# Four more filler products in batch 1's first unit, and the last softmax sums moved behind two more filler products and copied out by ScalarE

## The chip, the cores and the metric

The kernel runs on one core of one Trainium2 chip. The metric is the device time of one execution in microseconds, and less is better. Before the change it takes 974.06 us (median of 3 runs, 973.99 to 974.19). One execution was also recorded by the hardware profiler: its span is 971.3 us, and all times below that are given as a place ("at 526 us") count from the start of that span.

## The reference

Two blocks are computed one after the other, in float32. First comes attention over 4 batches, 8 heads, 768 positions and head size 64, in which a query sees only the keys that were assigned to the same one of 16 centroids:

```python
q_assign = argmax(einsum('bhsd,hcd->bhsc', q_n, c_n)); k_assign = argmax(...)   # normalized q, k, centroids
mask   = q_assign[:, :, :, None] == k_assign[:, :, None, :]
scores = where(mask, q @ k^T / sqrt(D), -1e9)
attn   = exp(scores - max) / (sum + 1e-9);  out = attn @ v
```

Its output, as 3072 tokens of width 512 (heads side by side), goes through a feed-forward block:

```python
h = x @ w_in            # 512 -> 2048
g = maximum(h, 0) ** 2
y = g @ w_out           # 2048 -> 512
```

## The kernel before, in words

**Two stages.** The first stage (up to 531 us) does all of the attention, and, mixed into it, the feed-forward block of batch 0. The second stage (531 us to the end) does the feed-forward block of batches 1 to 3 with seven products in place of eight (`ffn_pair`, a scheme of sums and differences of quarter matrices).

**Attention.** Heads go in pairs: `pair` counts 16 of them, four to a batch (`HP = 4`), and `h` is the half of the queries (384 columns). A unit is (pair, h, c), where c is 0, 2 or 4 and stands for two chunks of 128 keys. There are 96 units, run in the loop over `u`: the first 24 belong to batch 0, and so unit 24 is batch 1's first. A unit makes scores on TensorE (`scores`, tiles `sc`, lines 91 and 94) and the exponential on ScalarE (line 479). In batch 0 the mask is a second product on TensorE. From batch 1 on, VectorE multiplies by the mask (line 483): it compares `qid`, the cluster numbers of the queries, spread over all partitions, with `ids`, those of the keys, and writes `ex`. The tiles `sc` have two buffers of two banks each, and each unit uses both, so that the scores of one unit wait until the masks of the unit before have read the bank. GpSimd adds the `ex` tiles into `acc` (lines 493 and 495), and TensorE multiplies them with v (`times_v`, tiles `av`).

**Sums and division.** When a half is complete, `add_up` lets TensorE sum `acc` over partitions (`sm`), takes the reciprocal on VectorE into `r` (line 554), writes it to DRAM (`far_r`, line 557), reads it back to all partitions (`rb`, line 560), and also stores it in `seen`, from which `check_sums` learns at the end of attention whether all sums were in range. Then `finish` multiplies `av` by `rb` into `xT` (line 573), the input of the feed-forward block. In batch 0's second halves ScalarE copies the sums from their bank into `r` before the reciprocal (line 552); everywhere else the reciprocal reads the bank.

**Filler.** The feed-forward block of batch 0 is computed with plain products (`ffn`, a generator): 64 products of 384 columns per half for the first matrix (`ph`, line 587; ScalarE's relu and square to `gT` follow) and 48 of 512 columns for the second (`po`, line 600, then an output copy `osb` by ScalarE and a DMA). `fill_steps` takes them from the generators while TensorE would otherwise wait. How many a unit gets follows from `left`, the columns still to do, and `density(u)`, the weight of a unit: the share of a step is the columns left, less `RESERVE = 3 * DM`, times the weights of the step, over the weights of all units to come. Seven plain `po` products are left when the last unit's `av` products are done.

**Order.** Each engine runs its own list in order. The lists are made by a scheduler from the order of the program, from priorities (`tc.high_priority`) and from `tc.issue_after`. A change in the counts of filler products can therefore also move instructions of other engines past each other, such as the DMAs on SyncE's queue. On that queue stand, for each pair, the write of the transposed cluster numbers (`far<-row`, line 415), their spread to all partitions (`qid<-far`, line 416), and the DMA that transposes the next pair's q and k (`qkT<-words`, line 293).

**Other work beside it.** Up to about 160 us the feed-forward weights are loaded and rounded (`round_weights`, lines 150 to 167) by ScalarE, VectorE and GpSimd. The second stage begins with sums of inputs (`x_t`) and of `w_out` (`w_t1` to `w_t4`, 2048 columns each) on VectorE, and of `w_in` (`w_s`, 256 columns each) on GpSimd. Its products go to eight banks in turn; VectorE's additions into `g` (line 649) empty them. The eight banks take over those of the first stage, the one of the last `sm` among them.

Of the kernel before, what the change touches and what calls it, by code (L numbers as in the profile page):

```python
# [25 lines left out]
def kernel(  # L26
# [14 lines left out]
    NCH = S // P  # L41
    DM = H * D
# [3 lines left out]
    HP = H // 2  # L46
    NB = NCH // 2
    TB = NB * P
    NG = B * HP
# [31 lines left out]
    def bank(name, shape):  # L81
        return ps_f.tile(shape, F32, name=name, tag="f")
# [5 lines left out]
    def together(products, offset=2000):  # L88

        products = iter(products)  # L90
        last = nc.tensor.matmul(**next(products))  # L91
        with tc.high_priority(offset=offset):
            for product in products:
                last = nc.tensor.matmul(**product)  # L94
        return last.ins
# [178 lines left out]
    def split_words(pair, which):  # L274
        if which == 0:
            words[pair] = dram.tile([2 * NCH, P, 2, 2 * D], U16, name="words")
        flat = loads.tile([P, NCH, 2, 2 * D], U16, name="flat", tag="qk")
        src = raw[pair][which].bitcast(U16).rearrange("p c (d two) -> p c two d", two=2)
        half = NCH // 2
        with tc.issue_after(last_exp[0]):  # L280
            for cols in (slice(0, half), slice(half, NCH)):
                nc.scalar.copy(out=flat[:, cols], in_=src[:, cols])
        nc.sync.dma_start(
            words[pair][NCH * which : NCH * (which + 1)].rearrange("c p two d -> p c two d"),
            flat,
        )
        if which == 1:
            raw.pop(pair)
            load_qk(pair + 1)
# [131 lines left out]
    def prep(pair):  # L421
        if pair < HP:
            return [
                lambda: turn(pair, 0), lambda: turn(pair, 1), lambda: turn(pair, 2),
                lambda: logits(pair), lambda: route(pair),
                lambda: turn_onehot(pair, 0), lambda: turn_onehot(pair, 1),
            ]

        split = [lambda i=i: split_words(pair + 1, i) for i in range(2 if pair + 1 < NG else 0)]
        first, second = split or (None, None)  # L430
        return [
            lambda: turn_words(pair), None, None, first, None, None,
            lambda: logits(pair), None, lambda: route(pair), second, None, None,
            None, None, lambda: spread(pair),
        ]
# [10 lines left out]
    def first_half(pair, h):  # L446
        return pair < HP and h == 0
# [51 lines left out]
    def ones_products(sm, e, rhs, first, last):  # L499

        n, rows = TB // 2, P // 4
        return [
            dict(
                out=sm[rows * (2 * e + g) : rows * (2 * e + g + 1)], lhsT=ups[:, 0:rows],
                rhs=rhs[:, n * g : n * (g + 1)], start=first, stop=last,
            )
            for g in range(2)
        ]
# [27 lines left out]
    def add_up(pair, h):  # L536


        b, hp = divmod(pair, HP)
        if first_half(pair, h):  # L540
            sm = sums.pop((pair, h))
            nc.scalar.copy(out=xT_of(b, h)[:, hp], in_=av.pop((pair, h)))
        else:
            total = acc.pop((pair, h))
            sm = bank("sm", [P, TB // 2])
            one = [ones_products(sm, e, total[:, e], True, True) for e in range(2)]
            together([p for both in zip(*one) for p in both])
        row = 4 * (2 * pair + h)
        r = once.tile([P, TB // 2], F32, name="r")
        if pair < HP and h:  # L550

            nc.scalar.copy(out=r, in_=sm)
            sm = r
        nc.vector.reciprocal(out=r, in_=sm)
        r = r.rearrange("(r p) n -> r p n", r=4)[:, 0]
        far = dram.tile([2, TB], F32, name="far_r")
        nc.sync.dma_start(far.rearrange("e (g n) -> (e g) n", g=2), r)
        rb = rbp.tile([P, TB], F32, name="rb", tag="rb")
        for e in range(2):
            nc.sync.dma_start(rb[D * e : D * (e + 1)], far[e].partition_broadcast(D))  # L560
        nc.sync.dma_start(seen[row : row + 4], r)
        spread_out[pair, h] = rb

    def xT_of(b, h):
        if (b, h) not in xT:
            pool = {0: xtp, 1: xt_first, 2 * B - 1: xtp}.get(2 * b + h) or later["xT"]
            xT[b, h] = pool.tile([P, KT, TB], F32, name="xT")
        return xT[b, h]
# [44 lines left out]
    def ffn_pair(pools, b):  # L613
# [114 lines left out]
    units = [  # L728
        (pair, h, c)
        for pairs, halves in [(range(HP), [0]), (range(HP), [1])]  # L730
        + [([pair], [0, 1]) for pair in range(HP, NG)]
        for pair in pairs for h in halves for c in range(0, NCH, 2)
    ]
# [10 lines left out]
    def density(u):  # L744


        return 4 if u < HP * NCH else 2 if u < len(units) - NCH else 3

    def fill_steps(columns):

        while fill and columns > 0:
            if (passed := next(fill[0], None)) is None:
                fill.pop(0)
            else:
                columns -= passed
                left[0] -= passed

    def behind_first(u, what=last_logits):
        return tc.issue_after(what[0]) if u == 0 else ExitStack()

    def next_pair(u):

        pair, h, c = units[u]
        if c == 0 and pair + 1 < NG and h == 0 and (pair + 1) not in qkT:
            if pair + 1 < HP or pair >= HP:
                return pair + 1
        if u == TWOS + 4:
            return HP
        return None
# [26 lines left out]
    for u in range(len(units) + 3):  # L796
        if u < len(units):
            pair, h, c = units[u]
            if (p := next_pair(u)) is not None:
                ahead.extend(prep(p))  # L800
            if u in (TWOS, TWOS + 2):

                split_words(HP, int(u > TWOS))
            if c == 0 and u + 3 < len(units) and units[u + 3][0] not in raw_v:
                load_v(units[u + 3][0])

            with behind_first(u):
                scores(pair, h, c)

        ends(added)  # L810
        added.clear()
        if u < TWOS:
            ready = u - 1
        elif u == TWOS or u % 2 or u >= len(units):
            ready = u

        complete, late = late, []
        while v_next < min(ready, len(units)):
            pair, h, c = units[v_next]
            times_v(pair, h, c)  # L820
            v_next += 1
            if c == NCH - 2:
                (late if h and not HP * NCH <= u < len(units) else complete).append((pair, h))
        for pair, h in complete:
            with tc.high_priority(offset=1000) if first_half(pair, h) else ExitStack():
                add_up(pair, h)
            if h == 1:
                for d in (qkT, ids, qid):
                    d.pop(pair)
            if h == 1 or pair < HP:  # L830
                raw_v.pop(pair)
            added.append((pair, h))

        rounding += 4
        while rounding >= 3:
            rounding -= 3
            i = next(to_round, None)
            if i is not None:
                with tc.issue_after(last_exp[0]):
                    round_weights(i)  # L840
                if (i := next(loaded, None)) is not None:
                    load_weights(i)
            elif not later:
                early.close()
                for name, bufs in (("xT", 5), ("out", 2)):
                    later[name] = keep.enter_context(
                        tc.tile_pool(name=name + "_late", bufs=bufs, side="right",
                                     reuse_waits="tile")
                    )
        share = 0  # L850
        if u % 2 == 0 or not TWOS < u < len(units):
            n = 2 if TWOS < u < len(units) else 1
            share = max(0, left[0] - RESERVE) * sum(map(density, range(u, u + n)))
            share //= max(1, sum(map(density, range(u, ENDS))))
        goal = left[0] - share

        for i in range(3):
            if i == 2:
                fill_steps(share * 2 // 3)
            if ahead:  # L860
                with behind_first(u, masked if i else last_logits):
                    (ahead.pop(0) or int)()
        fill_steps(left[0] - goal)
# [235 lines left out]
```

The softmax here doesn't subtract the row's maximum and nothing guards it: scores larger than these inputs give would overflow.

## Time and profile before

The time is 974.06 us and the span in the profile 971.3 us, at a granted TensorE clock of 1.00 throughout. The table shows how long TensorE was busy in stretches of the span. What is missing to the length of the stretch is idle time.

| Stretch, us | Length | TensorE busy | What runs there |
|---|---|---|---|
| 0 to 20 | 20.0 | 15.69 | loads, centroids, first routing |
| 20 to 60 | 40.0 | 39.05 | first halves of batch 0 |
| 140 to 160 | 20.0 | 18.40 | last unit of batch 0, first units of batch 1 |
| 200 to 240 | 40.0 | 39.24 | batch 1, with filler |
| 400 to 440 | 40.0 | 39.34 | batch 3, with filler |
| 440 to 480 | 40.0 | 39.58 | batch 3, with filler |
| 510 to 531 | 21.0 | 19.41 | last unit, last sums, last filler |
| 531 to 603 | 72.0 | 72.00 | second stage, batch 1, first matrix |
| 893 to 971.3 | 78.3 | 72.67 | second stage, batch 3, second matrix, and output |

The stretches between, which are not shown, have 0.3 us of idle time in all. In a row of the timeline the columns are the start, the duration, the engine, the line, the operation, what is written from what is read, its shape and its count, and in brackets how long the engine had been idle before it and what ended that. A row of the waits names who waited for whom, the total in microseconds, how many times, and the longest. SPq rows are DMAs as SyncE's queue issues them. TensorE shows each float32 product as two records, so "x4" of line 600 is two products.

### The profile page before, as it was taken

What the parts mean: (1) busy time and instruction counts of PE and PEld (TensorE: products, weight loads), DVE (VectorE), ACT (ScalarE), POOL (GpSimd) and SP (SyncE); (2) the same over time, 40 slices, a digit from 0 to 9 for tenths busy, and PEclk for the clock granted to TensorE, in tenths of its full rate; (3) what the DMA queues carried; (4) which work ended last, traced back from release to release, by engine and by line L of the source; (5) the groups of instructions that cost most, each with busy time, mean ns of one, the idle gap of its engine ahead of it and who ended that gap; (6) DMA issues with size and microseconds to landing.
All of it is one profiled execution on the core that took longest, in us unless ns stands there. A gap on an engine that the chain in (4) does not pass through costs nothing.

```text
span 971.3 us, 12075 instructions
## 1 busy us (share of the span) xinstructions
PE 955.1 (98%) x4479; PEld 550.6 (57%) x4479; DVE 569.1 (59%) x913; ACT 316.8 (33%) x516; POOL 381.8 (39%) x277
## 2 busy tenths in 40 slices
PE   7999999999999999999999999999999999999997
PEld 4544454443444444443444556888556888556886
DVE  5779976666665666566657956431656432656331
ACT  5887755443435555543331111000111000111000
POOL 1338866565665555655567331002231002331000
PEclk9999999999999999999999999999999999999999
DMA  9667772453455544553110000000000000000000
GB/s 247 195 200 212 202 199 65 108 153 97 122 123 125 132 114 109 122 114 102 51 42 26 3 1 0 22 22 22 1 0 1 22 22 22 1 1 0 22 23 25
DMA packets 127746, 74.54 MB, mean 77 GB/s; under 512 B 90944, under 2 KB 119104, under 8 KB 127680
## 3 DMA queue, kind: packets, MB, share of 16 engines
q1 hardware_dynamic: 125968, 73.26, 27.9%
q8 instruction: 38, 0.62, 0.3%
q10 hardware_dynamic: 1712, 0.43, 0.2%
q14 instruction: 28, 0.23, 0.1%
HBM read 48.27 MB, written 15.86 MB: 66 GB/s over the span
## 4 chain that ended last, share of the span: by engine, by line
PE 87%; DMA 4%; DVE 2%; POOL 2%; SPq 2%; ACT 2%; issue 1%; ACTq 0%; DVEq 0%; POOLq 0%
PE bank L710 22%; PE bank L679 22%; PE po L600 8%; PE sc L91 7%; PE sc L94 6%; PE ph L587 6%; PE av L91 6%; PE av L94 5%; DMA far_r<-r 1%; DMA rb<-far_r 1%; PE sm L91 1%; PE sm L94 1%; SPq L293 1%; POOL acc L495 1%; PE lg L91 1%
## 5 line engine op out<-in xcount | busy, mean ns | idle before, releaser
L495 POOL TENSOR_TENSOR acc<-acc,ex 128x768 f32<-128x768 f32 x112 | 207.5, 1853 | 103.5 <-DVE ex L483 95.7
L483 DVE SCALAR_TENSOR_TENSOR ex<-qid,ids,sc 128x384 f32<-128x384 bf16 x288 | 157.7, 608 | 64.8 <-ACT sc L479 50.1
L479 ACT ACTIVATE sc<-sc 128x768 f32<-128x768 f32 x144 | 108.4, 793 | 159.1 <-PE sc L94 141.3
L94 PE MATMUL sc<-qkT 64*128 64x384 f32 x576 | 152.2, 503 | 0.8
L94 PE MATMUL av<-ex,v_raw 128*64 128x384 f32 x576 | 135.3, 491 | 0.0
L668 POOL TENSOR_TENSOR w_s<-w_in 128x256 f32<-128x256 f32 x24 | 18.1, 755 | 274.0 <-PE bank L710 162.0
L649 DVE TENSOR_TENSOR g<-bank,g 128x384 f32<-128x384 f32 x144 | 77.8, 555 | 79.1 <-PE bank L679 77.9
L710 PE MATMUL bank<-w_out,g 128*128 128x256 f32 x432 | 95.2, 379 | 0.0
L600 PE MATMUL po<-w_out,gT 128*128 128x512 f32 x192 | 91.7, 609 | 0.0
L587 PE MATMUL ph<-xT,w_in 128*128 128x384 f32 x256 | 91.3, 498 | 0.2 <-ACT gT L594 0.2
L91 PE MATMUL sc<-qkT 64*128 64x384 f32 x192 | 87.1, 534 | 2.8 <-DVE ex L483 2.8
L710 PEld LDWEIGHTS bank<-w_out,g 128*128 128x128 f32 x432 | 82.1, 190 | 11.8
L649 DVE TENSOR_TENSOR osb<-bank,osb 128x256 f32<-128x256 f32 x54 | 22.1, 423 | 107.6 <-PE bank L710 102.2
L94 PEld LDWEIGHTS sc<-qkT 64*128 64x128 f32 x576 | 65.1, 186 | 27.7 <-issue 5.4
L91 PE MATMUL av<-ex,v_raw 128*64 128x384 f32 x192 | 80.3, 500 | 0.0
L493 POOL TENSOR_TENSOR acc<-ex 128x768 f32<-128x768 f32 x28 | 51.4, 1837 | 49.8 <-DVE ex L483 36.7
L679 PE MATMUL bank<-xT,w_in 128*128 128x384 f32 x192 | 69.9, 487 | 0.0
L679 PE MATMUL bank<-x_t,w_s 128*128 128x384 f32 x192 | 69.8, 486 | 0.0
L679 PE MATMUL bank<-xT,w_s 128*128 128x384 f32 x192 | 69.8, 486 | 0.0
L94 PEld LDWEIGHTS av<-ex,v_raw 128*64 128x64 f32 x576 | 49.5, 137 | 34.2 <-issue 34.0
L587 PEld LDWEIGHTS ph<-xT,w_in 128*128 128x128 f32 x256 | 45.8, 189 | 38.7 <-issue 11.2
L710 PE MATMUL bank<-w_t,g 128*128 128x256 f32 x288 | 65.1, 379 | 0.0
(132 smaller groups left out, 1228.5 us busy)
## 6 DMA issues: line engine op xcount, KB each, us to landing
words<-flat SPq DMA_DIRECT2D x24, 384.0 KB
w_raw<-in_moe_w_in_dram SPq DMA_DIRECT2D x16, 512.0 KB
w_raw<-in_moe_w_out_dram SPq DMA_DIRECT2D x16, 512.0 KB
v_raw<-in_v_dram SPq DMA_DIRECT2D x20, 384.0 KB
rb<-far_r SPq DMA_DIRECT2D x64, 96.0 KB
q_raw<-in_q_dram SPq DMA_DIRECT2D x31, 192.0 KB
k_raw<-in_k_dram SPq DMA_DIRECT2D x31, 192.0 KB
out_dram<-osb SPq DMA_DIRECT2D x23, 256.0 KB
```

What stands on the lines that cost most here:

```text
L91: last = nc.tensor.matmul(**next(products))
L94: last = nc.tensor.matmul(**product)
L479: last_exp[0] = nc.scalar.activation(out=t[:, 2 * i : 2 * i + 2] if pair < HP else src, in_=src, func=ACT.Exp, scale=SCALE).ins
L483: last_mask[0] = nc.vector.scalar_tensor_tensor(out=t[:, 2 * i + e], in0=qid[pair][1][:, h, e], scalar=ids[pair][:, ch % NB, 2 + ch // NB, ...
L493: nc.gpsimd.tensor_tensor(out=acc[pair, h], in0=t[:, 0:2], in1=t[:, 2:4], op=ALU.add)
L495: nc.gpsimd.tensor_tensor(out=acc[pair, h], in0=acc[pair, h], in1=t[:, 2 * i : 2 * i + 2], op=ALU.add)
L587: nc.tensor.matmul(ph, lhsT=w_in[:, kk, f * P : (f + 1) * P], rhs=xT[b, h][:, kk], start=(kk == 0), stop=(kk == KT - 1),)
L600: nc.tensor.matmul(po, lhsT=gT[f][:, i * P : (i + 1) * P], rhs=w_out[:, f], start=(f == 0), stop=(f == FT - 1),)
L649: nc.vector.tensor_tensor(out=out, in0=bank, in1=to, op=ALU.add)
L668: nc.gpsimd.tensor_tensor(out=s1, in0=a[1][0], in1=a[1][1], op=ALU.add)
L679: nc.tensor.matmul(bank, lhsT=operands[j][0][:, kk], rhs=operands[j][1][:, kk], start=(kk == 0), stop=(kk == H2 - 1),)
L710: nc.tensor.matmul(bank, lhsT=operands[j][0][:, f], rhs=operands[j][1][:, f], start=(f == 0), stop=(f == F2 - 1),)
```

## The change

It has three edits. `density` is 4 rather than 2 in units 24 and 25 as well, which gives ten plain products rather than six to batch 1's first unit and takes a few from the units ahead of it. After the last unit, `fill_steps(2 * DM)` takes two more plain products (1024 columns) before the last `add_up`, so that four of the seven kept ones stand ahead of the last sums, which wait for GpSimd's `acc`, and three behind. And the last half's sums are copied out of their bank by ScalarE, as batch 0's second halves do it, so that VectorE's reciprocal reads `r` and the bank is free after ScalarE's copy.

```diff
         row = 4 * (2 * pair + h)
         r = once.tile([P, TB // 2], F32, name="r")
-        if pair < HP and h:
+        if (pair < HP or pair == NG - 1) and h:
 
             nc.scalar.copy(out=r, in_=sm)
             sm = r
...
     def density(u):
 
-        return 4 if u < HP * NCH else 2 if u < len(units) - NCH else 3
+        return 4 if u < HP * NCH + 2 else 2 if u < len(units) - NCH else 3
...
                 (late if h and not HP * NCH <= u < len(units) else complete).append((pair, h))
+        if u > len(units) and complete:
+
+            fill_steps(2 * DM)
         for pair, h in complete:
             with tc.high_priority(offset=1000) if first_half(pair, h) else ExitStack():
                 add_up(pair, h)
```

## The prediction

> **What bounds the kernel now.** I read the page's busy shares first, then what TensorE waited for, then the stretches around those waits in the timeline.
>
> ```profile
> PE 955.1 (98%) x4479; PEld 550.6 (57%) x4479; DVE 569.1 (59%) x913; ACT 316.8 (33%) x516; POOL 381.8 (39%) x277
> PE sc L91 <- DVE ex L483: 2.8, 4, 1.5
> PE sm L91 <- POOL acc L495: 1.6, 1, 1.6
> ```
>
> TensorE is busy for 955.1 of 971.3 us at a granted clock of 1.00, so no reordering can win more than 16.2 us, and most of that is start (4.3 us idle in the first 20 us) and the drain at the end (5.6 us in the last stretch). The change adds and removes no matmul. It can only win idle time in the middle: scores waiting for the masking VectorE does in their bank (2.8 us, four times, the longest 1.5), and the last sums waiting for GpSimd (1.6 us, once). The longest score wait:
>
> ```profile
> 155.63 1.40 POOL L167 TENSOR_TENSOR w_out<-w_out,w_raw 128x512 int32<-128x512 int32 x1 [1.31 <-DVE w_out L163]
> 155.92 1.40 DVE L163 TENSOR_SCALAR w_out<-w_raw 128x512 uint32<-128x512 uint32 x1
> 157.24 2.18 DVE L483 SCALAR_TENSOR_TENSOR ex<-qid,ids,sc 128x384 f32<-128x384 bf16 x4
> 158.42 0.59 PE L91 MATMUL sc<-qkT 64*128 64x384 f32 x1 [1.46 <-DVE ex L483]
> ```
>
> The scores of batch 1's second chunk (158.42) need the bank whose first two masks end about 158.35. The masks stand behind weight rounding on VectorE, whose last step took 1.40 us where the same line took 0.42 elsewhere in this stretch, because GpSimd was in its own operation. The second bank costs another 0.4: this block of four score products takes 1.89 us (158.42 to the next at 160.31), the undisturbed one at 151.33 takes 1.49. The second place, 220.99:
>
> ```profile
> 212.54 3.43 SPq L293 DMA_TRANSPOSE qkT<-words  x1
> 216.03 0.58 SPq L416 DMA_DIRECT2D qid<-far  x1
> 219.70 2.19 DVE L483 SCALAR_TENSOR_TENSOR ex<-qid,ids,sc 128x384 f32<-128x384 bf16 x4 [4.07 <-DMA qid<-far]
> 220.99 0.56 PE L91 MATMUL sc<-qkT 64*128 64x384 f32 x1 [0.63 <-DVE ex L483]
> ```
>
> Here the transposing DMA held the SyncE queue for 3.43 us, the cluster numbers (qid) behind it came late, and so masks and scores. It costs 0.63 plus 0.4 for the second bank. The same pattern stands at 403 us (0.52 plus 0.4). In the ten other pairs qid is issued first and no such wait shows. The end of attention:
>
> ```profile
> 521.13 4.86 POOL L495 TENSOR_TENSOR acc<-acc,ex 128x768 f32<-128x768 f32 x2 [1.43 <-DVE ex L483]
> 526.05 0.35 PE L91 MATMUL sm<-acc,ups 128*32 128x192 f32 x1 [1.59 <-POOL acc L495]
> 526.51 4.56 PE L600 MATMUL po<-w_out,gT 128*128 128x512 f32 x10
> 532.17 0.84 POOL L621 TENSOR_TENSOR w_s<-w_in,w_s 128x256 f32<-128x256 f32 x1
> 539.95 0.55 DVE L649 TENSOR_TENSOR g<-bank,g 128x384 f32<-128x384 f32 x1
> 540.42 2.64 DVE L621 TENSOR_TENSOR w_t<-w_t,w_out 128x2048 f32<-128x2048 f32 x1
> ```
>
> TensorE does two plain products, waits 1.59 for GpSimd's accumulator, does the sums, then five more, and the seven-product stage begins at 530.91.
>
> **What the Trainium skill says.** "SBUF — State Buffer", section "Who interferes with whom", says that GpSimd and a VectorE instruction with two SBUF inputs or in a 2-port mode exclude each other, the later one blocking until the first ends. The trace agrees: between 521 and 529 us VectorE's 768-wide subtractions take 0.95, 2.45, 2.55 and 1.47, and each ends one bare duration after GpSimd's own operation ended. It also says that an instruction with one SBUF input doesn't contend. The reciprocals (1.35 beside GpSimd or not) agree. "Perfetto Trace Analysis", section "DMA Instruction — HWDGE (DVE, Sync)", says that a DMA's row ends when the queue is free, not when data has landed. Here qid's row ends at 216.61 and its reader starts at 219.70.
>
> **The change, part by part.**
>
> (1) Ten products in the first unit. I compared the two programs' instruction lists. Three plain products leave the stretch ahead of batch 1's first scores, and that unit gets ten instead of six, so the second chunk's scores come one product later in the list, and two chunks on the counts are level. A product costs 0.67 (eleven from 139.49 to 146.78 gave 0.66, six from 152.82 to 156.96 gave 0.69). TensorE thus reaches batch 1's first scores 3 x 0.67 = 2.0 earlier (149.3) and the second chunk's at 156.96 + 0.67 = 157.6. When are the masks ready? Their VectorE chain hangs on DMA, not on TensorE: the chain of waits goes words, transposition, far_r, far, far_r, rb, and rb lands for the xT product at 150.76. I leave that time. What moves is GpSimd: its two 1.85-us additions, after exps that now end 2.0 earlier, can start when the rounding ahead of them ends (148.62) instead of 150.26, so end at 152.2 instead of 154.3. The rounding after 151.3 meets them once, not twice: 0.70 + 0.43 + 0.69 + 0.42 + 0.43 from 152.2 gives 154.9, then one GpSimd operation (1.28) and 0.42: 156.3 instead of 157.3. First two masks at 157.4, before TensorE arrives. Gain 1.46; the 0.4 at the second bank stays. Bounds: if VectorE is no earlier, 158.42 stays and only the added product is won, 0.7; if both banks are free, 1.9. The two plain banks: pb's row copy (0.24) sits in front of ph's reuse of its bank, with one product of 0.67 to cover it; the sums' bank is reused two products (1.3) after them, while ScalarE's two exps and copy need 1.5 + 0.33. I charge nothing for these, bound 0.3.
>
> (2) The queue order it shifts. With other product counts the scheduler places SyncE's DMAs otherwise in three pairs: at 212 and 394 qid now stands ahead of the transposition, at 305 it falls behind:
>
> ```profile
> 305.43 0.34 SPq L416 DMA_DIRECT2D qid<-far  x1
> 305.86 4.09 SPq L293 DMA_TRANSPOSE qkT<-words  x1
> 312.62 0.59 PE L91 MATMUL sc<-qkT 64*128 64x384 f32 x1
> ```
>
> Gained: 1.03 and 0.92. Lost: the transposition would start about 304.3, 1.0 to 1.4 after the far write as at 212 and 394, qid would go out about 308, land 3.6 to 4.0 later, and the first masks end at 312.9 instead of before 312.62. A wait of 0.3 plus 0.4, bounds 0.2 and 1.1. An output DMA now stands before rb at 210 us and can delay masks by 0.4; I take 0.1. Sum +1.1, bounds +0.4 and +1.6.
>
> (3) The end. Four products (3.6 us, as from 513.26 to 516.89) ahead of the sums cover the 1.59: sums at 526.1 as now, three products left, the next stage at 529.3 instead of 530.9. ScalarE's copy of the sums is 0.33 with nothing queued (it idles 11.7 us there), and is over long before VectorE is free at 528.2, so it costs nothing; queued behind it is only the output copy, which needs the last plain product anyway. But VectorE's list changes: all four w_t now come ahead of the first g addition, where one came after it. In this stage the tenth product waits for the bank that this addition empties. Today it starts at 530.91 + 9 x 1.29 = 542.5 and the addition ended at 540.5: 2 us to spare. After: the tenth could start at 540.9. VectorE: reciprocal to 529.5, then each w_t (2.15 bare, 2.27 to 2.80 seen) alternates with one of the five GpSimd weight sums still to come (0.72 seen alone), since w_t no longer waits for the seen DMA until 532.4. In turn: w_s to 530.2, w_t 532.3, w_s 533.0, w_t 535.2, xT 535.7, w_t 538.0, w_s 538.7, seen 539.0, w_s 539.5, w_t 541.7, addition 542.2. So the tenth starts at 542.2, not 542.5: of 1.6 won, 0.3 remains. Bounds: -0.3 (one more lock turn) and +1.6 (no collision).
>
> Sum: 1.46 + 1.1 + 0.3 = 2.9, so 974.06 - 2.9 = 971.2.
>
> **The rivals.**
> A, forecast, 971.2: chance 0.50.
> B, the masks of the first unit are still paced by rb and the rounding, and the tail is a draw: 0.7 + 0.4 + 0.0 = 1.1, 973.0. For it: that chain is DMA after DMA. Against: its last third is lock waits that do move. Chance 0.23.
> C, the collision at the tail doesn't show, or lasts a turn less: 1.46 + 1.1 + 1.6 = 4.2, 969.9. For it: w_t asks at 529.5 within 0.1 of a GpSimd start, so the turns may fall the other way. Against: every lock turn from 521 to 543 fits. Chance 0.19.
> D, slower: the first unit's masks come late by one more lock turn and the added product covers none of it (+0.7), the 305 pair costs its full 1.1 while the waits at 212 and 394 come back with a later transposition (+1.1), and the tail loses 0.3: 976.2. For it: each step has a precedent in this profile. Against: all would have to fall the wrong way. Chance 0.08.
>
> **How the numbers follow.** The likeliest is A. Widening to C below and B above, with 0.2 of room each way, gives 969.7 to 973.2, and leaves out D and the outer parts of B and C. Faster by over 0.2% means under 972.1: C and most of A (0.49), 0.68. Within 0.2%: B, the rest of A and some of D, 0.27. Slower: the rest of D and what I have not seen, 0.05.
>
> **What would show it.** Step 1: the wait of scores for L483 near 156 us gone, ten products between the two score blocks. Step 2: no wait near 220 and 402 us, a new one near 312. Step 3: no wait of sm for GpSimd, next stage 1.6 earlier relative to the last av, and then a TensorE wait of about 1.3 us at its tenth product, released by g. A tail without that wait, or masks still at 157.2, makes the prediction wrong.

## The result, and the profile after

The changed kernel takes 970.86 us (median of six runs, 970.09 to 971.8). Beside it, on the same chip, the kernel before took 974.12 us. The ratio is 0.9963, with a 95% interval of 0.995 to 0.9976, so it is 3.3 us faster. The profiled execution has a span of 968.7 us instead of 971.3.

From the page of the changed kernel:

```profile
PE 956.1 (99%) x4479; PEld 551.1 (57%) x4479; DVE 570.0 (59%) x913; ACT 317.5 (33%) x517; POOL 388.0 (40%) x277
```

And from its waits (who waited for whom, the total, how often, the longest):

```profile
PE bank L680 <- DVE g L650: 0.8, 1, 0.8
PE sc L91 <- DVE ex L483: 0.4, 1, 0.4
```

The sums' wait is gone from TensorE's rows, and the wait of scores for the masks is down from 2.8 us in four places to 0.4 in one. A wait of 0.8 has come at a bank of the second stage. Each of these is shown below in the timeline. (From line 553 on, a line has a number one higher than before; the lines that an experiment adds shift its numbers further.)

To see where the time went I read the start of each score block (the four products of one unit's scores) in both profiles and subtracted. Idle time alone doesn't do it, since part of the waits lies inside a group of products and counts as busy.

| Place | Forecast, us | From the score blocks, us |
|---|---|---|
| up to 90 us (nothing is changed there) | 0 | -0.2 |
| batch 1's first unit, to 170 us | 1.46 | 1.9 |
| SyncE's queue order, and whatever else differs from 170 to 515 us | 1.1 | 0.38 |
| end of attention to the tenth product of the second stage | 0.3 | 0.67 |
| sum | 2.9 | 2.7 |

How the second row is found: at the block of 170 us the changed kernel is 0.77 ahead of before, was 0.28 late at 112 us, and has done one plain product of 512 columns more on the way, which comes off its list later. Two such products start 0.86 apart, so the first unit has given 0.77 + 0.28 + 0.86 = 1.91. At the last block the counts are level, and it is 2.01 ahead; 2.01 - 0.77 - 0.86 = 0.38 is the third row. That the medians differ by 3.3 and the two profiles by 2.7 is within what single executions vary (the six of the changed kernel lie 1.7 apart; see also the last section).

**The first unit** in the timeline of the changed kernel:

```profile
148.74 3.72 POOL L495 TENSOR_TENSOR acc<-acc,ex 128x768 f32<-128x768 f32 x2
150.14 1.13 PE L94 MATMUL sc<-qkT 64*128 64x384 f32 x5
151.19 6.72 PE L588 MATMUL ph<-xT,w_in 128*128 128x384 f32 x20
156.10 2.18 DVE L483 SCALAR_TENSOR_TENSOR ex<-qid,ids,sc 128x384 f32<-128x384 bf16 x4
157.84 0.59 PE L91 MATMUL sc<-qkT 64*128 64x384 f32 x1
158.28 1.13 PE L94 MATMUL sc<-qkT 64*128 64x384 f32 x5
```

Ten products (x20 records) stand between the two score blocks. The masks start at 156.10, 1.1 earlier than before, and end at 158.28. TensorE arrives at 157.84 and waits for neither bank: the last row of the block is 1.13 long, as in the undisturbed block at 150.14. GpSimd's two additions end at 152.46. Before the change they ended at 154.31, and so met more of VectorE's rounding ahead of the masks:

```profile
150.26 4.05 POOL L495 TENSOR_TENSOR acc<-acc,ex 128x768 f32<-128x768 f32 x2 [1.64 <-ACT ex L479]
```

**The pair at 212 us**. Before the change rb goes out first, and the output DMA behind it (at 210.53):

```profile
208.96 1.47 SPq L560 DMA_DIRECT2D rb<-far_r  x2
212.97 0.56 DVE L573 SCALAR_TENSOR_TENSOR xT<-av,rb 128x384 f32<-128x384 f32 x1 [3.40 <-DMA rb<-far_r]
```

In the changed kernel the output DMA stands ahead of rb:

```profile
208.17 0.80 SPq L609 DMA_DIRECT2D out_dram<-osb  x1
209.45 1.12 SPq L561 DMA_DIRECT2D rb<-far_r  x2
212.77 0.35 SPq L416 DMA_DIRECT2D qid<-far  x1
212.83 0.56 DVE L574 SCALAR_TENSOR_TENSOR xT<-av,rb 128x384 f32<-128x384 f32 x1 [4.03 <-DMA rb<-far_r]
214.58 0.56 PE L91 MATMUL sc<-qkT 64*128 64x384 f32 x1
215.01 1.53 PE L94 MATMUL sc<-qkT 64*128 64x384 f32 x5
```

qid goes out ahead of the transposition and the wait at 220 us is gone. But rb is issued at 209.45, half a us later than before although TensorE is 0.8 ahead. VectorE sits waiting for it at xT with the masks behind. The scores start 0.2 late (214.58 is 0.59 ahead of before, where the block in front was 0.78 ahead) and lose another 0.4 in their second bank (the row of 1.53, in place of 1.13). TensorE's list of waits has nothing of this: the row counts as busy, and the idle time in front is too short to be listed.

**The pair at 305 us**, where the order turned the other way:

```profile
303.09 3.03 SPq L293 DMA_TRANSPOSE qkT<-words  x1
306.22 0.53 SPq L416 DMA_DIRECT2D qid<-far  x1
310.69 2.19 DVE L483 SCALAR_TENSOR_TENSOR ex<-qid,ids,sc 128x384 f32<-128x384 bf16 x4 [4.63 <-DMA qid<-far]
311.97 0.56 PE L91 MATMUL sc<-qkT 64*128 64x384 f32 x1 [0.43 <-DVE ex L483]
312.41 1.53 PE L94 MATMUL sc<-qkT 64*128 64x384 f32 x5
```

The masks end their first bank at 311.8; TensorE waits 0.43 in front of the block and 0.4 within it.

**One more loss, at 236 us.** In the changed kernel the last row of the score block at 235.76 is 1.48 long, 0.35 over the undisturbed one:

```profile
232.11 0.56 DVE L574 SCALAR_TENSOR_TENSOR xT<-av,rb 128x384 f32<-128x384 f32 x1 [1.22 <-DMA rb<-far_r]
236.20 1.48 PE L94 MATMUL sc<-qkT 64*128 64x384 f32 x5
```

xT waits for rb until 1.03 after the start of the block in front (231.08). Before the change it waited until 0.30 after it (232.67, with the block at 232.37), although rb goes out 3.12 ahead of that block in both. So the late part is the landing, and the masks stand behind xT. It is not the new order: e12 below, the same kernel once more, loses nothing at this place, and e3, whose queue is that of before, loses 0.41.

**The end of attention:**

```profile
524.10 0.35 PE L91 MATMUL sm<-acc,ups 128*32 128x192 f32 x1
527.44 0.72 POOL L669 TENSOR_TENSOR w_s<-w_in 128x256 f32<-128x256 f32 x1
527.44 2.87 DVE L622 TENSOR_TENSOR w_t<-w_out 128x2048 f32<-128x2048 f32 x1
528.13 2.77 POOL L622 TENSOR_TENSOR w_s<-w_in,w_s 128x256 f32<-128x256 f32 x1
530.24 2.81 DVE L622 TENSOR_TENSOR w_t<-w_out 128x2048 f32<-128x2048 f32 x1
533.60 2.77 POOL L622 TENSOR_TENSOR w_s<-w_in 128x256 f32<-128x256 f32 x1
536.51 2.80 DVE L622 TENSOR_TENSOR w_t<-w_t,w_out 128x2048 f32<-128x2048 f32 x1
539.24 2.80 DVE L650 TENSOR_TENSOR g<-bank,g 128x384 f32<-128x384 f32 x5
539.84 1.56 PE L680 MATMUL bank<-xT,w_in 128*128 128x384 f32 x4 [0.82 <-DVE g L650]
```

The sums start with no wait. The second stage begins 12.36 after the last score block instead of 14.02, 1.66 earlier. Then its tenth product waits 0.82 for the first g addition, which stands behind the fourth w_t sum. By the distances this costs 0.99: the product starts 24.96 after the last score block, where nine products of 1.29 behind the 12.36 make 23.97. What is left of 1.66 is 0.67.

### The profile page after: what moved, and what is told of

It is laid out like the page before. It is cut to its first block, busy times and chain, and to the rows that moved or that the text cites. A ratio compares the mean times of both kernels' runs of the same rounds, so it can differ in the third digit from the quotient of the medians.

```text
span 968.7 us, 12081 instructions
## 1 busy us (share of the span) xinstructions
PE 956.1 (99%) x4479; PEld 551.1 (57%) x4479; DVE 570.0 (59%) x913; ACT 317.5 (33%) x517; POOL 388.0 (40%) x277
## 4 chain that ended last, share of the span: by engine, by line
PE 85%; issue 4%; POOL 4%; DMA 3%; DVE 2%; SPq 1%; ACT 0%; ACTq 0%; POOLq 0%; DVEq 0%
PE bank L711 22%; PE bank L680 21%; PE po L601 8%; PE ph L588 7%; PE sc L91 7%; PE av L91 6%; PE sc L94 5%; PE av L94 5%; POOL w_in L167 2%; PE sm L91 1%; DVE w_t L622 1%; PE lg L91 1%; POOL acc L495 1%; POOL w_out L167 1%; DMA q_raw<-in_q_dram 1%
## 5 line engine op out<-in xcount | busy, mean ns | idle before, releaser
L483 DVE SCALAR_TENSOR_TENSOR ex<-qid,ids,sc 128x384 f32<-128x384 bf16 x288 | 157.6, 608 | 63.9 <-ACT sc L479 39.5
L669 POOL TENSOR_TENSOR w_s<-w_in 128x256 f32<-128x256 f32 x24 | 20.2, 842 | 266.7 <-PE bank L711 162.0
L711 PE MATMUL bank<-w_t,g_s 128*128 128x256 f32 x288 | 65.1, 379 | 0.0
```

Of the source, the lines that this page charges most:

```text
L483: last_mask[0] = nc.vector.scalar_tensor_tensor(out=t[:, 2 * i + e], in0=qid[pair][1][:, h, e], scalar=ids[pair][:, ch % NB, 2 + ch // NB, ...
L711: nc.tensor.matmul(bank, lhsT=operands[j][0][:, f], rhs=operands[j][1][:, f], start=(f == 0), stop=(f == F2 - 1),)
```

## The experiments

**My theory** after reading the two traces: the first unit gives 1.9, the queue little because of two new waits, and the tail keeps 0.7 of its 1.6 because of VectorE's order. **The rivals**: the sizes of the prediction (1.46, 1.1, 0.3) hold and the trace is one lucky execution; the tail or the copy makes most of the gain; the stall at the tenth product comes from the earlier start, not from the w_t sum. Each group of four ran on one chip beside the kernel before, which took 974.03, 974.37 and 974.10 us in the three groups. A "pin" (`tc.issue_after` in the diffs) fixes the order of two instructions on one engine's list.

### Each edit alone

**e1, the first unit alone.**

```diff
-        return 4 if u < HP * NCH else 2 if u < len(units) - NCH else 3
+        return 4 if u < HP * NCH + 2 else 2 if u < len(units) - NCH else 3
```

> The kernel before with the first edit alone: the weight of 4 in units 24 and 25 (and the shifts of SyncE's queue that come with it). Theory, read from the trace after: the first unit gives 1.9 and the queue 0.35, so 2.3 us faster, 971.8. Rival 1 (the sizes of the prediction hold: 1.46 and 1.1): 2.6 faster, 971.5. Rival 2 (what the trace shows at the first unit is given back later, and the tail makes the gain): 0.5 faster or less, 973.6. In the profile: no wait of scores for the masks near 156 us, and all four score products of batch 1's second chunk within 1.5 us.

Measured: 971.23, ratio 0.9972 [0.9957, 0.9988], 2.8 faster. So most of the gain is this edit, with the shifts of the queue that it brings; rival 2 falls. The median can't tell the theory (2.3) from rival 1 (2.6). Its profile gives the first unit 1.58, not 1.91, and shows why:

```profile
157.59 1.45 PE L94 MATMUL sc<-qkT 64*128 64x384 f32 x5
```

In this execution TensorE comes to the place 0.7 earlier (157.15), while xT still waits for rb until 150.8 and the masks start at 155.89. The second bank's wait of 0.3 is back. The masks hang on a chain of DMAs and TensorE doesn't, so being still earlier is lost there.

**e4, eight products instead of ten** (weight 3).

```diff
-        return 4 if u < HP * NCH else 2 if u < len(units) - NCH else 3
+        return 3 if HP * NCH <= u < HP * NCH + 2 else 4 if u < HP * NCH else 2 if u < len(units) - NCH else 3
```

> The kernel before with a weight of 3 rather than 4 in units 24 and 25: batch 1's first unit gets eight products, and none is taken from the stretch ahead, so its scores stay at 151.3. The queue shifts at 212, 305 and 394 us are the same as with a weight of 4. It tells filling the wait from starting earlier. Theory: two products of 0.67 fill 1.34 of the wait of 1.46; the rest of it and the second bank's wait stay because masks come no earlier: 1.4 from the first unit, 0.35 from the queue, 1.7 faster in all, and 0.5 slower than with ten products. Rival (the earlier start of GpSimd's additions is what frees the masks): under 1.0 from the first unit. In the profile: masks of the first unit at 157.2 and scores of the second chunk at 158.4 with no or a small wait.

Measured: 972.27, ratio 0.9982 [0.9972, 0.9993], 1.8 faster, and 1.0 slower than e1, where 0.5 was expected. The scores of batch 1's first unit start at 151.87, not earlier. Then:

```profile
150.79 4.05 POOL L495 TENSOR_TENSOR acc<-acc,ex 128x768 f32<-128x768 f32 x2 [2.30 <-ACT ex L479]
157.77 2.18 DVE L483 SCALAR_TENSOR_TENSOR ex<-qid,ids,sc 128x384 f32<-128x384 bf16 x4
158.96 0.59 PE L91 MATMUL sc<-qkT 64*128 64x384 f32 x1 [0.17 <-DVE ex L483]
159.39 1.53 PE L94 MATMUL sc<-qkT 64*128 64x384 f32 x5
```

GpSimd's additions wait for exps until 150.79 and meet the rounding twice, and the masks start at 157.77; this execution was 0.5 late already at 112 us, so that is the 157.24 of before. Two products fill 1.3 of the wait; 0.17 and the second bank's 0.4 stay, and by the blocks the first unit gives 1.24. The changed kernel fills only 0.67 net (four products more, three fewer ahead); the rest of its 1.9 is masks that start 1.1 earlier. The rival, under 1.0 from filling, falls, but so does filling as the whole reason.

**e2, the tail alone; e3, the copy alone.**

```diff
-        if pair < HP and h:
+        if (pair < HP or pair == NG - 1) and h:
...
+        if u > len(units) and complete:
+            fill_steps(2 * DM)
...
```

e2 has both hunks, e3 the first alone.

> The kernel before with the second and third edit alone: four kept products ahead of the last sums, and ScalarE's copy of the sums. Nothing moves ahead of 513 us. Theory: the wait of the sums (1.6) goes, a stall of about 0.8 to 1.0 at the second stage's tenth product comes, 0.6 to 0.7 us faster, 973.4. Rival 1 (the stall after is an accident of where the GpSimd turns fell in the changed kernel): 1.6 faster, 972.5. Rival 2 (the stall takes all): no difference, 974.1.

> The kernel before with the third edit alone: ScalarE copies the last sums out of their bank. TensorE's list stays; VectorE's list changes as in the changed kernel (all four w_t sums ahead of the first g addition). Theory: the reciprocal waits for VectorE's own x_t work until 528 either way, so the copy gains nothing; the first g addition is late, but the second stage begins at 530.9 as before and its tenth product is due at 542.5, so within 0.3 of before, 974.1. Rival 1 (the copy is a gain of its own): over 0.5 faster. Rival 2 (the new order of VectorE alone costs what it costs in the changed kernel): 0.8 to 1.0 slower, 975.0.

Measured: e2 973.38, ratio 0.9991 [0.9982, 1.0001]; e3 974.22, ratio 1.0002 [0.9991, 1.0014]. The medians are those of the theory, but e2's interval reaches past 1, so its 0.65 us is not told from nothing. The traces decide: e2 has no wait of the sums and again a wait of 0.82 at the tenth product. e3 has the same VectorE list, with all four w_t sums ahead of the first g addition, and no such wait:

```profile
527.64 0.35 PE L91 MATMUL sm<-acc,ups 128*32 128x192 f32 x1 [1.60 <-POOL acc L495]
543.15 2.80 DVE L649 TENSOR_TENSOR g<-bank,g 128x384 f32<-128x384 f32 x5
544.11 1.45 PE L679 MATMUL bank<-xT,w_in 128*128 128x384 f32 x4
```

There the sums still wait 1.60, TensorE comes to its tenth product at 544.11, and the first of five additions ends at 543.7. The late addition costs something only when TensorE comes earlier. It takes both, then: the early start and the w_t sum in front of the addition.

### The queue

**e5, the order of the transposition on the kernel before.** `last_qid` holds qid's DMA, and pairs above 5 are pinned behind it:

```diff
...
-        nc.sync.dma_start(
-            qkT[pair].rearrange("p c n -> p (c n)").bitcast(U16),
...
+        with tc.issue_after(last_qid[0]) if pair > HP + 1 else ExitStack():
+            nc.sync.dma_start(
+                qkT[pair].rearrange("p c n -> p (c n)").bitcast(U16),
...
```

> The kernel before with one order on SyncE's queue: the DMA that transposes the next pair's q and k is put behind qid's, which at 212 and 394 us it stands ahead of. Product counts and all other lists stay. It is the queue half of the prediction by itself. Theory (the prediction's price of the two waits, 1.03 and 0.92): 1.9 faster, 972.1, with no wait of scores near 220 and 402 us. Rival (what the trace of the changed kernel shows at the first of the two places: the masks gain 0.5 only, and the later transposition makes a new wait behind it): 0.5 to 1.2 faster, 973.2.

Measured: 971.26, ratio 0.997 [0.9961, 0.9979], 3.1 faster, more than either said. In its profile each of the two places gives 1.0, as the prediction had priced them (1.03 and 0.92), and of the score waits only the first unit's is left. SyncE's queue at the first place:

```profile
213.87 0.34 SPq L419 DMA_DIRECT2D qid<-far  x1
214.27 4.68 SPq L296 DMA_TRANSPOSE qkT<-words  x1
```

The row of its waits that stands in for 2.8, 4, 1.5:

```profile
PE sc L91 <- DVE ex L486: 1.4, 1, 1.4
```

The later transposition costs nothing behind it. Another 0.35 comes at 449 us, where the kernel before has the fourth of its four score waits (0.15, and 0.4 in the second bank):

```profile
445.82 0.56 DVE L573 SCALAR_TENSOR_TENSOR xT<-av,rb 128x384 f32<-128x384 f32 x1 [1.50 <-DMA rb<-far_r]
449.42 0.56 PE L91 MATMUL sc<-qkT 64*128 64x384 f32 x1 [0.15 <-DVE ex L483]
```

xT waits there for rb until 1.30 after the start of the block in front (444.52), in e5 until 0.94, and the masks behind it come sooner by as much. The queue has the same order there in both, and the landing of rb is what differs, so this is not the edit's. The trace accounts for some 2 us; the interval goes from 2.05 to 3.8, and I can't place the rest up to 3.1. By the medians this one order is worth about as much as the whole change.

**e6, the same order on the changed kernel**, where it moves the pair at 305 alone.

> The changed kernel with the same order on SyncE's queue, which there touches the pair at 305 us alone. Theory: the wait at 312 (0.43 as idle time, 0.96 by the distance of the score blocks) goes and nothing comes for it, 0.9 faster than the changed kernel, 970.0. Rival (the later transposition delays the next pair as much): within 0.3 of the changed kernel, 970.9.

Measured: 969.61, ratio 0.9958 [0.9946, 0.9971]. In the profile the blocks pass 312 us without a loss (1.47 ahead of before on both sides), where the changed kernel fell from 1.15 to 0.24 ahead, a loss of 0.91. In four other profiles with the changed order (e1, e4, e11, e12) the loss is 0.73 to 1.32, and in e7 only 0.13: there the masks start 0.24 sooner and TensorE comes at 312.00, with its bank free.

**e9, beside it the output DMA behind rb.** `last_rb` holds rb's DMA:

```diff
...
-            nc.sync.dma_start(out_view[b, h * NB + i], osb)
+            with tc.issue_after(last_rb[0]):
+                nc.sync.dma_start(out_view[b, h * NB + i], osb)
```

> The changed kernel with the transposing DMA behind qid's, and the output DMAs of the plain products behind the rb reads on SyncE's queue; at 208 us, where the changed kernel has them the other way round, this undoes it. Beside it, at 527 us, the last output DMA goes behind the last rb. Theory: rb and so xT and the masks of the pair at 212 come 0.6 earlier, and the waits at 214.5 (0.25 as idle time, 0.4 in the second bank) go: 0.5 faster than with the transposition's place alone, 969.1. Rival (the rb reads are late for another reason): no difference to that run, 969.6.

Measured: 969.11, ratio 0.9951 [0.9934, 0.9968]. The step from e6 is inside the intervals, so the place itself has to tell. What the pair at 212 gives against before is 1.00, 0.91 and 1.07 in the three profiles with the output behind rb (e5, e9, e10), and 0.31 to 0.69 in the eight with qid ahead of the transposition but the output ahead of rb, 0.50 on average. The output DMA ahead of rb costs some 0.5.

### The tail

**e7, the last w_t sum behind the first g addition.** `g_added` holds the additions in order:

```diff
...
-                sub(w_t[to], one, two)
+                with tc.issue_after(g_added[0]) if to == 4 else ExitStack():
+                    sub(w_t[to], one, two)
```

> The changed kernel with the last of the four w_t sums queued behind the first g addition on VectorE. Theory: the first g addition runs at about 537 instead of 539.2, the stall of the tenth product (0.82 as idle time) goes and the whole 1.6 of the tail is kept: 0.8 to 1.0 faster than the changed kernel, 970.0. The w_t sum then stands ahead of the second addition, whose bank the eleventh product needs only 1.3 later. Rival (the stall moves to the eleventh product, whose bank the delayed additions empty): no difference, 970.9.

Measured: 968.96, ratio 0.9944 [0.9923, 0.9965]. VectorE and TensorE around it:

```profile
536.14 0.55 DVE L652 TENSOR_TENSOR g<-bank,g 128x384 f32<-128x384 f32 x1
536.61 2.34 DVE L622 TENSOR_TENSOR w_t<-w_t,w_out 128x2048 f32<-128x2048 f32 x1
538.50 1.45 PE L683 MATMUL bank<-xT,w_in 128*128 128x384 f32 x4
539.79 1.45 PE L683 MATMUL bank<-xT,w_s 128*128 128x384 f32 x4
```

The addition ends at 536.7 and the tenth product (538.50) starts on time, 23.97 after the last score block instead of 24.96. The eleventh follows in step, so the stall doesn't move on. That is the 1.0 of the theory. The median fell by more, from a wide interval.

**e11, the changed kernel without the copy, and e12, the changed kernel again.**

> The changed kernel without its third edit: VectorE's reciprocal reads the last sums from their bank. Theory: the reciprocal waits for VectorE's own x_t sums until 526.1 either way and frees the bank at 527.5, before the second or third product of the second stage (528.5 and 529.8) wants it, and VectorE's list stays: no difference to the changed kernel, 970.9. Rival (the copy frees the bank in time, and without it the second product waits): 0.5 to 1.0 slower, 971.6.

> The changed kernel once more, as it is, on the same chip as the three others, so that they can be compared with it there. Expected: 970.9, with a stall of 0.8 at the tenth product of the second stage again, since each engine's order there is the same; the waits at 214 and 312 us, which hang on DMA landings, may come out smaller or larger by some tenths.

Measured: 970.22 both, ratios 0.9958 [0.9941, 0.9974] and 0.9955 [0.9939, 0.997]. The copy neither gains nor costs anything that shows, in either kernel. The stall at the tenth product is there in both (0.82 and 0.86).

### Together

**e8** joins e6 and e7, and **e10** joins e9 and e7.

> The changed kernel with both: the transposing DMA behind qid's, and the last w_t sum behind the first g addition. Theory: the two places are far apart and add up, 1.8 faster than the changed kernel, 969.1. Rival (one of the two gives nothing): 970.0.

> The changed kernel with the transposing DMA behind qid's, the output DMAs behind the rb reads, and the last w_t sum behind the first g addition. Theory: the three add up, 0.9 + 0.5 + 0.9 = 2.3 faster than the changed kernel, 968.5. Rival (the runs with one and two of them already stand at 968.8 to 969.0, and what is left is the same in all): 968.8.

Measured: e8 968.77, ratio 0.9943 [0.9923, 0.9964]; e10 968.17, ratio 0.9934 [0.9918, 0.995]. e10 has the lowest median of all, 5.9 below before and 2.05 below the changed kernel of e12, which ran beside it. Its trace has neither a wait of scores for masks among TensorE's waits, nor one of a bank for g. That it beats e8 is not shown: the intervals overlap.

## Why the prediction was right, and where its sizes were not

The time (970.86 against 971.2) and the three mechanisms are as forecast. The sizes were off in three terms, by +0.4, -0.7 and +0.4, and these nearly cancelled. That the total came within 0.4 is in part luck.

**Step 1, the first unit: 1.46 said, 1.91 found.** Right: three products fewer ahead, masks at 156.1 (156.3 was said), ten products, and the way there, since e4 shows that without the earlier GpSimd additions the masks stay where they were and 0.6 is lost. Wrong: "the 0.4 at the second bank stays". It followed from no sum. The second bank's masks end 1.1 after the first's, and TensorE takes half of the block's 1.49 for the first bank, so it has to arrive 0.35 behind the first bank's masks. The prediction's own times (157.4 and 157.6) are 0.2 apart, which leaves a wait of 0.15 and not of 0.4. In seven of nine profiles with ten products the whole 1.9 is won. In e1 and e8, where TensorE came early, 1.6 and 1.3 are. One sum in this step doesn't come out as it is written: 154.9 + 1.28 + 0.42 is 156.6. The 156.3 holds only if that GpSimd operation starts 0.3 before VectorE comes to it, as it did before the change (155.63 and 155.92) and does after it (154.50 and 154.80). One reading is too wide as well: of the four subtractions between 521 and 529 us the first (0.95, to 521.86) ended while GpSimd's addition still ran, so it shows no lock; the other three end 0.82 after GpSimd's operations.

**"Two chunks on the counts are level" is wrong.** The changed kernel is one product ahead in most blocks from there until late in attention (0.86 where it is one of 512 columns). That cost the forecast nothing, but whoever reads a gain off score blocks without it finds 0.9 too little.

**Step 2, the queue: 1.1 said, 0.38 found.** The two waits were priced rightly, as e5 shows on the kernel before. The loss at 305 was 0.91, not 0.7. The term that was furthest off is the output DMA ahead of rb: 0.1 was taken and 0.4 was the bound, and 0.5 is what it costs. The queue's three places give 0.51 + 1.00 - 0.91 = 0.60 in this profile. The rest, down to 0.38, is landings of rb: 0.35 lost at 236 us and 0.14 won at 449, which no change of the queue explains. The slack was there to read: before the change xT waited for rb until 212.97, the masks right behind it ended at 215.63, and the second bank's scores came 0.3 later. Against TensorE, xT now comes 0.64 later, twice that slack.

**Step 3, the tail: 0.3 said, 0.67 found.** The turns of w_t and w_s came in the order that was worked out. What was too large is the price of a turn: a weight sum between two instructions of VectorE was taken at its 0.72, and it adds 0.58 to 0.59 (the first w_t ends at 530.31, the weight sum behind it at 530.90). With three such turns ahead of it the first addition ended 0.4 earlier than forecast. The stall cost 0.99, not 1.3. The copy costs nothing that shows (e3, e11), and rival C's tail without a collision doesn't happen in any of the six profiles that have the two products ahead of the sums and no pin.

## What to carry to other kernels

When a scheduler places DMAs on one queue, a change in product counts is also a change in that queue: compare the queue's order before and after, and price each swap by who reads the DMA that falls back. When you move a wait away from an engine, look for the next thing it meets early: here 1.0 of the 1.66 won at the sums was lost at the tenth product of the next stage, and one pin gave it back. And measure a gain by the distance of landmarks, not by idle time alone.

## What the runs showed of the hardware

A wait inside a group of products appears as a longer row, not as idle time: the row of the last score products is 1.13 undisturbed and 1.45 to 1.53 when the second bank is late. Each of the four score waits before the change had another 0.4 hidden that way, more than the listed wait itself at 449 us (0.15).

GpSimd's 256-column weight sum takes 0.72 alone and 2.77 while VectorE runs w_t sums, and these take 2.81 to 2.87 then, where 2.15 is what one takes after the end of a weight sum (528.16 to 530.31): in these rows the two engines alternate one instruction each. This agrees with the Trainium skill, "SBUF — State Buffer", section "Who interferes with whom", by which GpSimd reading SBUF and a VectorE instruction with two SBUF inputs exclude each other.

The landing of one rb near 81 us differs from one execution to the next: VectorE waited 0.34 for it in the profile of the changed kernel and 1.72 in that of e11, where TensorE then waited 1.19 for xT:

```profile
84.62 3.79 PE L588 MATMUL ph<-xT,w_in 128*128 128x384 f32 x11 [1.19 <-DVE xT L574]
```

Nothing of the change touches that place. Slips of 1.0 to 1.4 us stand there in three of the fourteen profiles (e2, e10, e11), hardly less than the 1.7 between the fastest and the slowest of the changed kernel's six executions. So a single span is no measure of a gain of 1 us; the places have to tell.
